# Linear attention and maxout feed-forward: keys' maximum taken off on VectorE, turned keys over two PSUM banks, order by new numbers

## The chip, the cores and the metric

One core of a Trainium2 chip. The core has TensorE (PE in the profile: matrix products and transposes; PEld is its weight load), VectorE (DVE), ScalarE (ACT), GpSimd (POOL) and SyncE (SP), which here only issues DMAs; ScalarE issues some too. The metric is the device time of one execution, in microseconds (us). The kernel before takes 657.2 us, the median of three runs (656.23 to 659.95).

## The reference

Eight batches of eight heads, 576 tokens, head size 64. Queries go through a softmax over the head's 64 columns, keys through one over the 576 tokens; then two small products per head, and a feed-forward with three gates of which the largest is kept:

```python
q_s = np.exp(q - np.max(q, axis=-1, keepdims=True))
q_s = q_s / (np.sum(q_s, axis=-1, keepdims=True) + 1e-09)
k_s = np.exp(k - np.max(k, axis=2, keepdims=True))
k_s = k_s / (np.sum(k_s, axis=2, keepdims=True) + 1e-09)
kv = np.einsum('bhsd,bhse->bhde', k_s, v)
x = np.einsum('bhsd,bhde->bhse', q_s, kv)        # 4608 tokens x 512, heads side by side
h = np.maximum(np.maximum(x @ w1, x @ w2), x @ w3)   # d_ff 768
return (h @ w_out).astype(np.float32)
```

q, k and v are float32; the four weights arrive as float64.

## The kernel before

**Stages.** Tokens are worked on in chunks of 512 columns. A product of float32 accuracy is made of three float32r products of a high and a low part (line 972: low by high, high by low, high by high). Chunks 0 to 2 run plain (`Chunk`, gates at line 973, second layer at 1012); the other six go in three duos that save products by adding blocks first (`Duo`, lines 1149 and 1260). The weights come as twelve slices of 1 MB. Each slice is turned from float64 into high and low parts by a run of steps (`Slice`): line 510 or 508, 512, 514 and 518 on VectorE (the first may go to ScalarE), 541 and 537 on ScalarE, 532 on GpSimd, 551 on VectorE or GpSimd. A gate needs its slice split and its chunk's x.

**Attention.** `Pair` is two heads of a batch, so 32 pairs. Batches 0 and 1 (eight pairs) are "turned": they run while the weights still arrive. For these, `k_turned` transposes the keys on TensorE into PSUM (L644 four blocks of 128 tokens, L650 the last 64), takes the maximum along the tokens on VectorE (L655 to L657), makes the exponentials on ScalarE with that maximum as bias (L663, L664, with the sum as a by-product), transposes them back (L671, L673), copies them out (L680), and multiplies with v (L722, ten products of 64x64). The result, scaled by one over the sum (L728, L731), is written into two diagonal blocks of a 128x128 tile `bdf` (L734). Queries are normalized in rows (L748 to L801), transposed (L830), copied out (L835), and L846 makes x for 512 columns as one 128x512 product. L854 and L856 split x into high and low parts. The other 24 pairs are "plain" (`k_plain`, `Quad`), with lines 687 to 707 and 880 to 929; they run beside the gates.

**PSUM.** Seven banks of 512 columns are handed out by the planner; the eighth, `ps`, is cut in quarters that take turns for the last 64 keys (L650), the last block of the turned-back exponentials (L673), the product with v (L722) and others.

**Order.** Every engine executes its own list of instructions in order. The lists are written by a planner (`Streams`), which runs through the steps of all parts by a cost for each step and a rank; tables of numbers at the head of the file (`LATE`, `AT`, `Q_OFF` and so on) are the ranks. Where the planner sees TensorE idle for more than 0.35 us in the first 110 us of its own clock, it writes fillers: products of 128x128 with the identity whose result nobody reads (L460), about one per 0.26 us of that gap (`fill`). The numbers of the fillers are therefore fixed when the program is written. `Q_BY_ACT` names the pairs whose query exponentials ScalarE makes row group by row group (L764, eight for a turned pair) in place of a subtraction on VectorE (L769), one exponential (L793) and a sum on VectorE (L795).

Of the kernel before, what the change touches and what calls it, by code (L numbers as in the profile page):

```python
# [48 lines left out]
SLICES_AT = -84.14
SLICE_STEP = 134.98  # L50
SLICE_HI = -258.29
SLICE_LO = 126.09
GATES_AT = -85.68
FIRST_LOADS = 'kqKkwqvqvKqkvVwvVk'
FIRST_ON_ACT = 9
LEFT_AT = -128.94
ROOMS = 2, 2, 2, 2

Q_BY_ACT = (1, 2, 6, 7, 8, 9, 10, 11, 12, 14, 17, 18, 20, 24, 25, 27, 31)

PLAIN = 3
FIRST_BANKS = 5
# [63 lines left out]
def dve_reduce(n):  # L126
    return (n + 140) / 960


def act(n):  # L130
    return n / 1200 + 0.12
# [181 lines left out]
def linear_attention_then_maxout_ffn(  # L313
# [48 lines left out]
    ps = ctx.enter_context(tc.tile_pool(name="ps", bufs=1, space=PSUM))  # L362
# [20 lines left out]
    banks = [pf.tile([P, CH], F32, name=f"bank{i}") for i in range(7)]  # L383
# [12 lines left out]
    bdf = [start.tile([P, P], F32, name=f"bdf{i}", bufs=1) for i in range(TURNED * NP)]  # L396
    qbuf = [start.tile([P, 2, 4, D], F32, name=f"q1{i}", bufs=1) for i in range(2)]

# [13 lines left out]
    for i in reversed(range(TURNED * NP)):  # L412
        nc.gpsimd.memset(bdf[i], 0.0)
    for i in range(2):
        nc.gpsimd.memset(vbuf[i][:, :, :, D:NV], 1.0)
        nc.gpsimd.memset(vbuf[i][LEFT:P, :, 4, :], 0.0)
# [15 lines left out]
    def banks_of_heads(key):  # L432
        return (4, 5, 6) if key[-1] < NP * (PLAIN + 2) else range(7)
# [4 lines left out]
    for d in range((B + 1 - PLAIN) // 2):  # L438
# [3 lines left out]
        {"pf": banks_of_gates, "pa": banks_of_heads, "ring": RING, "ws": 1, "sums": 1, "vs": 1, "halves": 2, "ps": 4, "keT": ROOM_KET, "hp": NJ, "tmp": N_TMP, "ke": 2, "qe": ROOM_QE, "qf": ROOM_QF, "qt": 2, "tb": N_TB, "qT": N_QT},  # L442
# [23 lines left out]
    class Slice:  # L466
# [35 lines left out]
        def join(self, room):  # L502
            n, low, high = self.n, self.low, self.high
            e = yield Step("AV", (1.0, 0.67), [("wst", n)], take=[(room, n)], port="V")
# [6 lines left out]
            yield Step("V", 0.67, port="V")  # L511
            nc.vector.tensor_scalar(out=x, in0=x, scalar1=HIGH_LEAST, scalar2=HIGH_MOST, op0=ALU.max, op1=ALU.min)
# [53 lines left out]
    class Pair:  # L566
# [70 lines left out]
        def k_turned(self):  # L637
# [9 lines left out]
            if n == 0:  # L647
                filler(0, 7, 1.0)
# [931 lines left out]
```

## Time and profile before

| | |
|---|---|
| median of 3 runs | 657.2 us (656.23 to 659.95) |
| profiled execution: span from first to last instruction | 653.8 us; the median of the runs is 3.4 us more |
| TensorE busy | 642.4 us (98%), 3594 matmul records |
| VectorE busy | 452.2 us (69%) |
| ScalarE busy | 289.5 us (44%) |
| GpSimd busy | 58.7 us (9%) |
| DMA | 140.64 MB, 215 GB/s in the mean |
| granted TensorE clock, mean | 0.997 |

The profile gives no time of the profiled execution other than its span, so what lies around the span is the difference to the runs: 2.4 to 6.1 us. A busy engine in the profile is one that runs an instruction; fillers count as busy. A float32 product is recorded as two matmuls, a float32r product or a transpose as one. The mean of a matmul is longer than its share of the time because matmuls overlap; the chain of waits gives each its own share.

### The profile page before, as it was taken

The numbers are of one execution on the slowest core, as the hardware profiler recorded it, in microseconds if no ns is written. First come the engines' busy times: TensorE is split into PE (matmuls) and PEld (weight loads), VectorE is DVE, ScalarE is ACT, GpSimd is POOL, SyncE is SP. The second block draws the span as 40 slices with busy tenths as digits, with TensorE's granted clock in tenths as the row PEclk, the third lists the DMA queues.
The fourth block names the chain that finished last, engine by engine and source line by source line (L and its number), as shares of the span: only waits on it lengthen the run. The fifth ranks groups of instructions, "written<-read, shape, count | busy, mean of one in ns | idle before, by whom it ended". The sixth has DMA issues, their size and how long they took to land.

```text
span 653.8 us, 9984 instructions
## 1 busy us (share of the span) xinstructions
PE 642.4 (98%) x3594; PEld 520.8 (80%) x3594; DVE 452.2 (69%) x788; ACT 289.5 (44%) x728; POOL 58.7 (9%) x72
## 2 busy tenths in 40 slices
PE   9899999999999999999999999999999999999997
PEld 9678778888777787777877787888888888888885
DVE  7899778688998898998999792253548614444521
ACT  5877584377663774664535354111113421111132
POOL 1322433201010100000000000000000000000000
PEclk9899999999999999999999999999999999999999
DMA  8999994378879997888997853466650536663012
GB/s 249 280 313 319 293 361 153 108 248 264 260 258 320 334 285 254 279 290 249 310 304 233 254 191 115 148 208 186 195 181 20 190 117 202 186 204 112 0 66 64
DMA packets 97953, 140.64 MB, mean 215 GB/s; under 512 B 28656, under 2 KB 57072, under 8 KB 96752
## 3 DMA queue, kind: packets, MB, share of 16 engines
q1 hardware_dynamic: 93008, 134.31, 65.5%
q10 hardware_dynamic: 4896, 5.70, 2.9%
q8 instruction: 28, 0.46, 0.3%
q14 instruction: 21, 0.17, 0.1%
HBM read 102.24 MB, written 37.75 MB: 214 GB/s over the span
## 4 chain that ended last, share of the span: by engine, by line
PE 79%; DMA 10%; DVE 6%; ACT 2%; issue 2%; SPq 1%; DVEq 0%; ACTq 0%
PE bank L1149 36%; PE bank L973 15%; PE bank L1260 15%; PE bank L1012 4%; DMA scratch<-bench 3%; DMA turned<-tb 2%; PE ps L880 1%; PE bank L460 1%; DMA wst<-in_moe_w_dram 1%; PE ps L722 1%; DMA kt<-in_k_dram 1%; PE bank L846 1%; DVE tb L806 1%; DMA gw<-scratch 1%; PE bank L929 1%
## 5 line engine op out<-in xcount | busy, mean ns | idle before, releaser
L1149 PE MATMUL bank<-gw 128*128 128x512 f32 x1134 | 261.3, 390 | 1.9 <-DMA gw<-scratch 1.3
L1149 PEld LDWEIGHTS bank<-gw 128*128 128x128 f32 x1134 | 212.1, 188 | 51.2 <-DMA gw<-scratch 2.1
L973 PE MATMUL bank<-gw 128*128 128x512 f32 x432 | 103.3, 395 | 0.0
L973 PEld LDWEIGHTS bank<-gw 128*128 128x128 f32 x432 | 80.2, 188 | 20.0 <-issue 3.6
L1260 PE MATMUL bank<-oh,halves 128*128 128x512 f32 x288 | 88.7, 389 | 0.0
L1260 PEld LDWEIGHTS bank<-oh,halves 128*128 128x128 f32 x288 | 54.1, 188 | 11.2
L1260 PE MATMUL bank<-ol,halves 128*128 128x512 f32 x144 | 56.3, 391 | 0.0
L973 PE MATMUL bank<-x,gw 128*128 128x512 f32 x216 | 50.1, 390 | 0.0
L973 PEld LDWEIGHTS bank<-x,gw 128*128 128x128 f32 x216 | 40.4, 188 | 9.2 <-issue 0.8
L1238 DVE TENSOR_TENSOR halves<-hf,halves 128x768 fp32r<-128x768 f32 (+2 forms) x30 | 23.7, 794 | 34.2 <-ACT halves L1236 34.2
L1012 PE MATMUL bank<-oh,h 128*128 128x512 f32 x144 | 44.4, 389 | 0.0
L782 ACT ACTIVATE qt<-qt,qm 128x64 f32<-128x64 f32 x117 | 39.2, 337 | 3.0 <-DVE qm L777 2.7
L1211 ACT COPY m<-bank 128x512 f32<-128x512 f32 x18 | 10.6, 588 | 61.7 <-PE bank L1149 59.2
L694 POOL PARTITION_ALL_REDUCE kma<-kh x24 | 18.9, 789 | 204.7 <-DVE ke L700 102.1
L1279 ACT COPY m<-bank 128x512 f32<-128x512 f32 x23 | 13.5, 589 | 52.4 <-PE bank L1260 52.4
L1260 PEld LDWEIGHTS bank<-ol,halves 128*128 128x128 f32 x144 | 27.0, 188 | 7.2 <-issue 0.8
L1206 ACT COPY m<-bank 128x512 f32<-128x512 f32 x18 | 10.6, 588 | 48.7 <-PE bank L1149 48.7
L985 DVE TENSOR_TENSOR m<-bank,m 128x512 f32<-128x512 f32 x36 | 24.7, 685 | 10.7 <-PE bank L973 7.9
L1012 PEld LDWEIGHTS bank<-oh,h 128*128 128x128 f32 x144 | 27.0, 188 | 5.6
L806 DVE STREAM_TRANSPOSE tb<-qt 128x576 f32<-128x576 f32 x24 | 30.4, 1273 | 0.1
L1213 DVE TENSOR_TENSOR m<-bank,m 128x512 f32<-128x512 f32 x18 | 12.4, 690 | 25.9 <-PE bank L1149 25.4
L1012 PE MATMUL bank<-ol,h 128*128 128x512 f32 x72 | 28.3, 393 | 0.0
(164 smaller groups left out, 883.4 us busy)
## 6 DMA issues: line engine op xcount, KB each, us to landing
gw<-scratch SPq DMA_DIRECT2D x75, 512.0 KB, 3.9
gw<-scratch SPq DMA_DIRECT2D x39, 256.0 KB, 3.7
wst<-in_moe_w_dram SPq DMA_DIRECT2D x9, 1024.0 KB, 7.1
scratch<-bench SPq DMA_DIRECT2D x9, 1024.0 KB, 5.3
out_dram<-m SPq DMA_DIRECT2D x32, 256.0 KB, 2.3
scratch<-gw SPq DMA_DIRECT2D x27, 256.0 KB, 3.4
qt<-in_q_dram SPq DMA_DIRECT2D x24, 288.0 KB, 4.3
kt<-in_k_dram SPq DMA_DIRECT2D x24, 256.0 KB, 4.8
```

What stands on the lines that cost most here:

```text
L694: nc.gpsimd.partition_all_reduce(kma, kmv.rearrange("p h d -> p (h d)"), P, bass_isa.ReduceOp.max)
L782: nc.scalar.activation(out=rows3[:, i, :], in_=rows3[:, i, :], func=AF.Exp, bias=qm[:, i : i + 1], accum_out=sums[:, i, 0:1],)
L806: nc.vector.transpose(out=tb.rearrange("p e (c s) -> p s e c", s=QS), in_=self.qt.rearrange("p s (c e) -> p s e c", e=2))
L973: nc.tensor.matmul(out=ps, lhsT=l[:, cc], rhs=r, start=(cc == 0 and t == 0), stop=(cc == NC - 1 and t == 2))
L985: nc.vector.tensor_max(out=m, in0=self.m.pop((j, i)), in1=m)
L1012: nc.tensor.matmul(out=po, lhsT=l, rhs=r[:, j, :], start=(j == 0 and i == 0), stop=(j == NJ - 1 and i == 2))
L1149: nc.tensor.matmul(out=po, lhsT=w[:, a, cc], rhs=x[:, b, cc], start=(first and cc == 0 and t == 0), stop=(cc == 1 and t == 2), skip_group_ ...
L1206: nc.scalar.copy(out=mb, in_=po("v"))
L1213: nc.vector.tensor_sub(out=ma, in0=po("w"), in1=ma)
L1238: nc.vector.tensor_sub(out=hl, in0=src, in1=hh.bitcast(F32))
L1260: nc.tensor.matmul(out=po, lhsT=l, rhs=r[:, j, :], start=(j == 0 and i == 0), stop=(end and i == 2))
L1279: nc.scalar.copy(out=o, in_=po)
```

## The change

- **Keys of a turned pair.** `KEYS_LESS` names the seven of eight pairs for which the maximum no longer becomes the bias of exponentials in the turned layout. After the turn and the maximum (one reduction over 576 columns), TensorE spreads the maximum over all partitions (L669: the maximum as a broadcast weight times the identity), VectorE subtracts it from the keys in token rows (L673, 128x640, in1 from PSUM), and ScalarE makes one exponential of 640 columns (L678). The transposes back and the copies out are gone for these. The sums come from five products with a column of ones (L739).
- **PSUM.** The eight banks are one tile, `psum`. The turned keys lie in one stretch of 576 columns, all of bank 6 and 64 columns of bank 7, always there; the product with v and the sums take banks 4 or 5. Filler, `ps` quarters and the rest are as before.
- **x.** `bdf` is 128x64, both heads' blocks below each other, written by one ScalarE instruction (L757). x is made by two products of 64x512 (L877). For three pairs (`X_LESS`) the low part of x is made on TensorE by subtracting the high part (L888) and a ScalarE copy, in place of VectorE's subtraction.
- **Slices.** The step at line 523 (512 before) may go to GpSimd.
- **Order.** All tables of ranks, `Q_BY_ACT` (turned pairs 0, 2 to 7 in place of 1, 2, 6, 7; fifteen plain pairs in place of thirteen), the order of the first loads, the banks and several costs of the planner are new. 57 fillers are written in place of 92.

```diff
-FIRST_LOADS = 'kqKkwqvqvKqkvVwvVk'
+FIRST_LOADS = "KqqkwKVkvvqvkVvqwk"
-FIRST_BANKS = 5
+FIRST_BANKS = 4
+HEADS_ON = 4, 5
+KEYS_LESS = (1, 1, 1, 1, 1, 1, 1, 0)
+X_LESS = (0, 1, 0, 1, 1, 0, 0, 0)
 def act(n):
-    return n / 1200 + 0.12
+    return n / 1200 + 0.07
...
+    turning = psum[:, 6 * CH : 6 * CH + S]
+    quarters = psum[:, 7 * CH :].rearrange("p (a b) -> p a b", a=4)
...
-            yield Step("V", 0.67, port="V")
-            nc.vector.tensor_scalar(out=x, in0=x, scalar1=HIGH_LEAST, scalar2=HIGH_MOST, op0=ALU.max, op1=ALU.min)
+            e = yield Step("VG", (0.61, 1.1), port="VG")
+            unit[e].tensor_scalar(out=x, in0=x, scalar1=HIGH_LEAST, scalar2=HIGH_MOST, op0=ALU.max, op1=ALU.min)
...
+            less = KEYS_LESS[n]
+            room = [("pa", ("kT", n)), ("last", ("kT", n))]
+            yield Step("T", 0.74, [("k", n)], take=room + ([] if less else [("keT", n)]), gives=None if less else ("ksub", n))
...
+            yield Step("V", dve_reduce(S), free=room[1:] if less else ())
+            km = att.tile([P, 1], F32, name="km2", bufs=4)
+            nc.vector.tensor_reduce(out=km, in_=turning, op=ALU.max, axis=AX.X, negate=not less)
+            if less:
+                yield Step("T", 0.25)
+                kb = turning[:, :P]
+                nc.tensor.matmul(out=kb, lhsT=km.broadcast_to([P, P]), rhs=ident, start=True, stop=True)
+                yield Step("V", dve(640), take=[("ke", n)], free=room[:1], gives=("ksub", n))
...
+                    op=ALU.subtract,
+                )
+                yield Step("A", act(640))
+                nc.scalar.activation(out=ke, in_=ke, func=AF.Exp)
+                return
...
+            if less:
+                yield Step("T", 0.35, [self.ago("xmm", 0)], take=last, gives=("sum", n))
+                kv = banks[st.bank(*last[0])]
+                for s in range(5):
+                    rows = slice(0, LEFT if s == 4 else P)
+                    nc.tensor.matmul(
+                        out=kv[:, D:NV], lhsT=ke[rows, s].rearrange("p h d -> p (h d)"), rhs=ones[rows],
+                        start=(s == 0), stop=(s == 4),
+                    )
...
-            nc.tensor.matmul(out=xT, lhsT=self.terms[0], rhs=self.terms[1], start=True, stop=True)
-            yield from x_words(b, self.g, xT, room)
+            less = bool(X_LESS[n])
+            for r in heads:
+                nc.tensor.matmul(
+                    out=xT[r], lhsT=self.terms[0][r], rhs=self.terms[1][r], start=True, stop=not less,
+                    skip_group_check=less,
+                )
...
+            yield Step("T", f32r(CH))
+            nc.tensor.matmul(out=xT, lhsT=minus, rhs=h, start=False, stop=True, skip_group_check=True)
```

How the lists read now, at three places. TensorE before, from behind the first turned query to the first x (`ps` takes the last keys and the product with v):

```order
L460 MATMUL bank_81<-ident 128x128 x13
L644 MATMUL bank_85<-ident,k_99 128x128 x4
L650 MATMUL ps<-ident,k_99 128x64
L460 MATMUL bank_81<-ident 128x128 x8
L722 MATMUL ps<-v_101,ke 64x64 x10
L671 MATMUL bank_86<-ident,keT 128x128 x4
L673 MATMUL ps<-ident,keT 64x128
L644 MATMUL bank_87<-ident,k_99 128x128 x4
L650 MATMUL ps<-ident,k_99 128x64
L460 MATMUL bank_81<-ident 128x128 x5
L846 MATMUL bank_85<-qf,bdf_102 128x512
```

and the same stretch of the change (`km` is the maximum, `zero` and `ident` with L471 the fillers):

```order
L859 MATMUL psum<-ident,qe 128x128 x4
L471 MATMUL psum<-ident 128x128
L657 MATMUL psum<-ident,k_90 128x128 x4
L657 MATMUL psum<-ident,k_90 128x64
L471 MATMUL psum<-ident 128x128 x3
L739 MATMUL psum<-ones,ke 128x1 x5
L752 MATMUL psum<-v_92,ke 64x64 x10
L471 MATMUL psum<-ident 128x128 x7
L669 MATMUL psum<-ident,km_329 128x128
L471 MATMUL psum<-ident 128x128
L877 MATMUL psum<-qf,bdf_93 64x512 x2
```

The transposes back (L671, L673) are gone, the spread of the next pair's maximum and the five sums are there, and the fillers between the first turned query and the first x fell from 26 to 12. Before that query stand 27 fillers before and 28 now.

VectorE before, from the first maximum of the keys on (`left<-wst` is the first weight slice):

```order
L655 TENSOR_REDUCE km_247<-bank_85 128x1
L656 TENSOR_REDUCE km_247<-ps 128x1
L657 TENSOR_SCALAR km_247<-km_247 128x1
L795 TENSOR_REDUCE qs<-qe 128x8
L797 TENSOR_REDUCE qr_145<-qs 128x8
L798 RECIPROCAL qr_145<-qr_145 128x8
L801 TENSOR_TENSOR qe<-qe,qr_145 128x512
L510 TENSOR_SCALAR left<-wst 128x1024
```

and of the change:

```order
L665 TENSOR_REDUCE km_241<-psum 128x1
L826 TENSOR_REDUCE qr_130<-qs 128x8
L827 RECIPROCAL qr_130<-qr_130 128x8
L824 TENSOR_REDUCE qs<-qe 128x8
L521 TENSOR_SCALAR left<-wst 128x1024
L830 TENSOR_TENSOR qe<-qe,qr_130 128x512
L523 TENSOR_SCALAR left<-left 128x1024
L673 TENSOR_TENSOR ke<-k_90,psum 128x640
```

The first step of the slice (L521) now stands ahead of the first pair's query scaling (L830) and of its key subtraction (L673); before, the query scaling (L801) stood ahead of the slice.

TensorE before, around the fourth x and the first keys of batch 1 (`kt`):

```order
L644 MATMUL bank_86<-ident,kt_92 128x128 x4
L650 MATMUL ps<-ident,kt_92 128x64
L846 MATMUL bank_85<-qf,bdf_105 128x512
L460 MATMUL bank_83<-ident 128x128 x8
L973 MATMUL bank_83<-gw 128x512 x3
L973 MATMUL bank_81<-gw 128x512 x3
L973 MATMUL bank_82<-gw 128x512 x3
L973 MATMUL bank_83<-gw 128x512 x9
L973 MATMUL bank_84<-gw 128x512 x12
```

and of the change:

```order
L877 MATMUL psum<-qf,bdf_96 64x512 x2
L657 MATMUL psum<-ident,kt_82 128x128 x4
L657 MATMUL psum<-ident,kt_82 128x64
L1016 MATMUL psum<-gw 128x512 x6
L888 MATMUL psum<-gw,minus 128x512
L471 MATMUL psum<-ident 128x128 x2
L669 MATMUL psum<-ident,km_590 128x128
L471 MATMUL psum<-ident 128x128
L739 MATMUL psum<-ones,ke 128x1 x5
L752 MATMUL psum<-vt_85,ke 64x64 x10
L1016 MATMUL psum<-gw 128x512 x6
```

Before, a run of 66 gate products follows here and batch 1's keys come later; now batch 1's pairs go on at once, with gates between them in sixes. When the last turned x is issued, 180 gate products lie behind it before and 96 now.

## Rows read from the trace of the kernel before

**Rows 1.** Stages: length; PE, PEld, DVE, ACT, POOL busy (instructions); clock; DMA; GB/s.

```profile
0.00:10.00 10.00, 8.93 (x58) 8.74 (x59) 7.07 (x23) 3.19 (x7) 2.02 (x17) 1.00 0.77 233
10.00:20.00 10.00, 7.44 (x70) 7.01 (x70) 8.63 (x17) 8.80 (x38) 2.54 (x2) 0.96 1.00 306
20.00:42.00 22.00, 21.93 (x176) 16.52 (x174) 19.54 (x42) 17.36 (x41) 6.96 (x6) 0.94 0.95 266
42.00:60.00 18.00, 18.00 (x93) 15.09 (x93) 16.77 (x27) 10.87 (x17) 4.44 (x4) 1.00 1.06 373
60.00:101.00 41.00, 39.65 (x268) 31.82 (x268) 33.27 (x65) 30.48 (x80) 15.13 (x12) 1.00 0.94 310
101.00:130.00 29.00, 29.00 (x140) 24.27 (x139) 21.98 (x32) 10.10 (x14) 9.49 (x10) 1.00 0.32 108
130.00:270.00 140.00, 140.00 (x917) 111.41 (x916) 122.90 (x246) 88.12 (x277) 11.79 (x14) 1.00 0.87 278
270.00:380.00 110.00, 108.07 (x648) 84.86 (x648) 100.08 (x178) 54.94 (x152) 6.35 (x9) 1.00 0.90 270
```

**Rows 2.** Groups on TensorE, 0 to 101 us: busy, mean ns, idle before.

```profile
L973 PE MATMUL bank<-gw 128*128 128x512 f32 x181 | 44.7, 400 | 0.0
L460 PE MATMUL bank<-ident 128*128 128x128 f32 x168 | 22.1, 280 | 0.0
...
L460 PE MATMUL bank<-bdf 128*128 128x128 f32 x16 | 3.8, 431 | 1.1 <-POOL bdf L413 1.1
```

**Rows 3.** Waits of TensorE, 0 to 101 us: total, times, longest.

```profile
PE ps L722 <- ACT keT L664: 2.6, 1, 2.6
PE ps L722 <- DVE km L656: 1.2, 3, 0.5
PE bank L460 <- POOL bdf L413: 1.1, 1, 1.1
```

**Rows 4.** Chain of waits: start us, us, what (x: records).

```profile
37.43 2.74 PE bank L973 x12
...
58.66 0.44 PE bank L671 x4
59.10 0.11 PE ps L673
...
60.95 0.95 PE ps L722 x20
...
69.19 1.53 PE bank L460 x12
...
86.60 0.86 PE bank L846 x2
```

**Rows 5.** TensorE in order of time: first key turn; a plain pair's x.

```profile
4.64 1.06 PE L644 MATMUL bank<-ident,k 128*128 128x128 f32 x4
...
208.19 1.09 PE L929 MATMUL bank<-qT,bd 64*64 64x64 f32 x10
```

**Rows 6.** VectorE in order of time: the first slice step.

```profile
11.20 0.69 DVE L510 TENSOR_SCALAR left<-wst 128x1024 uint32<-128x1024 uint32 x1 [1.42 <-DMA wst<-in_moe_w_dram]
```

**Rows 7.** Groups on VectorE by form (L700 over the whole span).

```profile
L518 DVE SCALAR_TENSOR_TENSOR left<-wst,left 128x1024 uint32<-128x1024 uint32 x6 | 7.6, 1273 | 0.0
L801 DVE TENSOR_TENSOR qe<-qe,qr 128x512 f32<-128x512 f32 x8 | 6.3, 791 | 0.0
...
L655 DVE TENSOR_REDUCE km<-bank 128x1 f32<-128x512 f32 x8 | 5.4, 670 | 0.1
L512 DVE TENSOR_SCALAR left<-left 128x1024 f32<-128x1024 f32 x7 | 4.8, 685 | 0.0
...
L700 DVE TENSOR_TENSOR ke<-kt,kma 128x640 f32<-128x640 f32 x24 | 19.4, 809 | 0.0
```

**Rows 8.** Groups on ScalarE and GpSimd by form, 0 to 101 us.

```profile
L764 ACT ACTIVATE qe<-q,qm 128x64 f32<-128x64 f32 x32 | 10.7, 338 | 0.0
...
L532 POOL TENSOR_TENSOR m<-left,wst 128x512 int32<-128x512 int32 x12 | 15.7, 1326 | 36.2 <-DVE left L518 13.2 <-ACT bdf L734 10.9 <-DMA kt<-in_k_dram 5.8
```

More of the change, by code (lines that the diff above doesn't have):

```diff
@@ L382, in linear_attention_then_maxout_ffn @@
     wholes = dram.tile([NG // 2, P, 2, CH], F32, name="wholes")
-    banks = [pf.tile([P, CH], F32, name=f"bank{i}") for i in range(7)]
+    psum = pf.tile([P, 8 * CH], F32, name="psum")
+    banks = [psum[:, i * CH : (i + 1) * CH] for i in range(7)]
     ident = const.tile([P, P], F32, name="ident")
@@ L395, in linear_attention_then_maxout_ffn, with flat_keys @@
     v0 = early.tile([P, H, 5, D], F32, name="v0")
-    bdf = [start.tile([P, P], F32, name=f"bdf{i}", bufs=1) for i in range(TURNED * NP)]
+    bdf = [start.tile([P, D], F32, name=f"bdf{i}", bufs=1) for i in range(TURNED * NP)]
+    zero = start.tile([P, P], F32, name="zero", bufs=1)
     qbuf = [start.tile([P, 2, 4, D], F32, name=f"q1{i}", bufs=1) for i in range(2)]
+    def flat_keys(t):
+        return t.rearrange("p h s d -> p (h s d)").rearrange("p (s h d) -> p s h d", s=5, h=2)
     nc.vector.memset(ones, 1.0)
@@ L411, in linear_attention_then_maxout_ffn @@
         )
-    for i in reversed(range(TURNED * NP)):
-        nc.gpsimd.memset(bdf[i], 0.0)
+    minus = start.tile([P, P], F32R, name="minus", bufs=1)
+    nc.vector.tensor_scalar(out=minus, in0=ident, scalar1=-1.0, scalar2=None, op0=ALU.mult)
+    nc.gpsimd.memset(zero, 0.0)
+    nc.gpsimd.memset(k0[LEFT:P, 4], 0.0)
     for i in range(2):
-        nc.gpsimd.memset(vbuf[i][:, :, :, D:NV], 1.0)
-        nc.gpsimd.memset(vbuf[i][LEFT:P, :, 4, :], 0.0)
+        nc.gpsimd.memset(flat_keys(kbuf[i])[LEFT:P, 4], 0.0)
     def main_rows(src, b, hs):
@@ L516, in join @@
             )
[L517 removed]
+            yield Step("V", 1.15, gives=("or", n), port="V")
             nc.vector.scalar_tensor_tensor(
@@ L639, in k_turned @@
             n, kt = self.n, self.kt
-            rooms = [("pa", ("kT", n)), ("ps", ("kTl", n))]
-            yield Step("T", 0.74, [("k", n)], take=rooms + [("keT", n)], gives=("ksub", n))
-            kT = banks[st.bank("pa", ("kT", n))]
-            for s in range(4):
+            less = KEYS_LESS[n]
[3 more added lines that the diff above has]
+                rows = slice(0, LEFT if s == 4 else P)
@@ L668, in k_turned @@
+            yield Step("A", act(S) + 0.2, free=room, gives=("sum", n))
+            keT = start.tile([P, S], F32, name="keT", bufs=ROOM_KET)
+            self.sums = start.tile([P, 1], F32, name=f"ks{n}", bufs=1)
+            nc.scalar.activation(out=keT, in_=turning, func=AF.Exp, bias=km, accum_out=self.sums)
+            rooms = [("pa", ("ke", n)), ("last", ("kel", n))]
             yield Step("T", 0.56, take=rooms + [("ke", n)], free=[("keT", n)])
@@ L714, in k_steps @@
                 return
-            ke = self.ke
-            last = [("ps", ("kv", n))]
-            yield Step("T", 0.9, [("v", n), self.ago("xmm", 0)], take=last, free=[("ke", n)], gives=("kv", n))
-            kv = next(small)
+            ke, less = self.ke, KEYS_LESS[n]
+            last = [("pa", ("kv", n))]
+            if less:
+                yield Step("T", 0.35, [self.ago("xmm", 0)], take=last, gives=("sum", n))
+                kv = banks[st.bank(*last[0])]
+                for s in range(5):
+                    rows = slice(0, LEFT if s == 4 else P)
+                    nc.tensor.matmul(
+                        out=kv[:, D:NV], lhsT=ke[rows, s].rearrange("p h d -> p (h d)"), rhs=ones[rows],
+                        start=(s == 0), stop=(s == 4),
+                    )
+                self.sums = kv[:, D:NV]
+            yield Step(
+                "T", 0.9, [("v", n), self.ago("xmm", 0)], take=[] if less else last, free=[("ke", n)], gives=("kv", n)
+            )
+            if not less:
+                kv = banks[st.bank(*last[0])]
             for s in range(5):
```

128 lines of the change are left out of this document (65 added, 63 removed).

## The prediction

> **What bounds the kernel now.** I read the stages first. From 101 to 270 us TensorE is busy without a gap, and from 270 to 380 it lacks 1.9 us [rows 1]; there the time is the number of products, and the change neither adds nor removes a gate product or a plain pair. Idle TensorE stands at the start: of the first 101 us it is busy 95.95, so 5.05 us are lost. The waits name them [rows 3]: 1.1 us for the first tile, 2.6 us at the first product of keys with v, put down to ScalarE's exponentials of the *next* pair (L664), and 1.2 us in three waits of the same product for VectorE's maximum of the last 64 keys (L656). These exponentials and maxima read other quarters of the PSUM bank that the product writes; the product does not need their data.
>
> But busy isn't useful. The groups of the first 101 us [rows 2] hold 25.9 us of fillers (22.1 and 3.8), which only stand where the planner saw a gap. So some 31 us of the first 101 are waiting of one kind or the other. Gates have 181 records; at 2.74/12 = 0.228 us of the chain each [rows 4] that is 41.3 us, and 101 - 41.3 - 25.9 - 5.05 = 28.7 us are left for the eight turned pairs. All the change can save lies in the 31 us of waiting and these 28.7 us. After 101 us it can only disturb.
>
> **The change part by part.** Each term goes against the profiled execution (span 653.8 us; the runs' median of 657.2 us is 3.4 more, which I keep).
>
> *Fillers.* 57 in place of 92, counted in the two lists. Six take 1.53 us in the chain [rows 4], 0.255 each: 35 x 0.255 = -8.9 us. This is only a gain where the wait behind them is gone too; real waits are a term of their own below.
>
> *Turned keys.* Seven pairs lose four transposes back (0.44) and the last block (0.11) [rows 4]: -3.9 us. They gain one product that spreads the maximum (128 columns, float32, as a filler: 0.255): +1.8. They gain five sums of one column. No row has such a shape. Its bounds are a 64x64 product, 0.95/10 = 0.095 us, and a filler with the same 128x128 weight, 0.255 [rows 4]; I take the transposes' 0.11, the nearest with a full weight: 35 x 0.11 = +3.9 (3.3 to 8.9).
>
> *x.* Three subtractions by product: 3 x 0.228 = +0.7. The two 64x512 halves in place of one 128x512 product use different quarters of the array. For a plain pair four such 64x512 products and one small one end within 1.09 us [rows 5], against 0.86 for one full float32 product [rows 4], so halves do run beside each other: 0. The bound is 0.86 more per pair.
>
> Work on TensorE together: -3.9 + 1.8 + 3.9 + 0.7 = +2.5 us.
>
> *Other engines.* VectorE is busy 78.2 of the 91 us from 10 to 101, ScalarE 67.5 [rows 1], so their sums matter. VectorE per turned pair: the maximum in one instruction saves two small ones, about 0.3, and the subtraction of 640 adds 0.81 [rows 7]: +0.5 x 7. Less: three low parts of x (0.7 each), three more queries by ScalarE (two operations of 0.7), three slice steps to GpSimd (0.685 each [rows 7]): -8.4. Sum about -5 us. ScalarE gains three queries at 8 x 0.338 = 2.7 [rows 8] less 0.6, and loses exponentials, copies back and one of two scalings in seven or eight pairs: about -2 us. Both get a little lighter: 0, hidden under TensorE. The three GpSimd steps are bounded by VectorE's 0.685 and twice GpSimd's 512-column addition, 2.65 us [rows 8]; the next step of that slice waits for it, but not the gates, of which only 96 are asked for by the last turned x, against 180 before. I cost it at 0; without that cover it is up to 3 x 2 = 6 us.
>
> *ScalarE's queue at the start.* It now issues five loads; two wait for an earlier load to land, and the first eight query exponentials stand behind them. The result is wanted only behind the first slice step on VectorE, which starts at 11.20 [rows 6]. Hidden: 0, at worst about 1.
>
> *Waits that go.* The product with v has a bank of its own: the 2.6 and the 1.2 us [rows 3] lose their cause. What is late next is worked out along the lists:
> - First turned query. VectorE's list has the slice step (11.20 to 11.89 [rows 6]) ahead of the query scaling (0.79 [rows 7]): ready at 12.7. TensorE turns the first keys at 4.64 [rows 5], 1.3 us with the last block, then comes 20 fillers and the spread later, 21 x 0.255 = 5.4: at about 11.3. Wait 1.4.
> - Second keys' turn. It overwrites the bank from which VectorE subtracts the first maximum, after a slice step: 12.7 + 0.69 + 0.81 = 14.2 [rows 7]. TensorE is there at 12.7 + 0.44 + 0.26 = 13.4. Wait 0.8.
> - Third. Between the two subtractions VectorE has one slice step of 0.69, one of 1.27, a query scaling 0.79, two reductions 1.4 [rows 7], small ones 0.7, two splits of 0.8 and the subtraction: 7.3 us, to 21.5. TensorE has from 14.2 on 14 fillers (3.6), turn, sums, product with v, spread, x and query, 0.65 + 0.55 + 0.95 + 0.255 + 0.86 + 0.44: 21.5 less what waits in between. Wait 0.7 with the spread's own.
> - Later turns in the same way: of the five left I take 3.3 us together, the largest at batch 1's first pair, whose turn stands straight behind the fourth x.
>
> With 1.1 at the start: 7.3 us, against 5.05: +2.2. First x should be out at about 20 us.
>
> *Steady part.* The first plain product stands behind 381 gate products in both lists. VectorE is busy 123 of 140 us there [rows 1], and two more of 24 plain queries go to ScalarE. The new order could remove the 1.9 us or double it: 0, bounds -2 and +4.
>
> Sum: -8.9 + 2.5 + 2.2 = -4.2 us. 657.2 - 4.2 = **653.0 us**. Ends, each alone: sums at the filler's price +5, halves one after another +6.9, GpSimd +6, steady part -2 to +4, waits at zero after the start -6.2.
>
> **The rivals.**
>
> *The wait stays, only the fillers go.* The 35 fillers stood for gaps the planner saw; its new costs may simply see shorter ones. For it: the 2.6 us wait of before was not planned, and VectorE at 86% leaves it little to catch up with. Against: the transposes back and their copies, two steps of the chain of each pair, are really gone. Half of the 8.9 us coming back as idle gives 657.4.
>
> *More overlap than I count.* If the turns find VectorE ahead, the waits shrink to the 1.1 and 1.4, 2.5 in place of 7.3 (-4.8), and the steady part gives its 1.9: 653.0 - 6.7 = 646.3. For it: VectorE gets 5 us lighter. Against: subtraction and maximum of a pair are now two stops in its list where there was one.
>
> *One bank for all turned keys (slower).* Before, L644 took one of several banks (87 and 86 in the lists above); now each turn waits until VectorE has subtracted for the pair before, behind whatever slice work is listed ahead. If each of seven waits holds a slice run of 0.685 + 0.685 + 1.27 = 2.64 us [rows 7], that is 18.5 in place of my 4.8: 666.7. It decides from 1.8 us a turn (4.8 + 7.5 over seven), where the sum passes 660.5. For it: the last of the lists has a turn straight behind x. Against: VectorE's list puts the subtraction near the front each time.
>
> *The halves of x take turns (slower).* Both halves now write one bank, on different partitions; in the plain pairs' rows each row half has a bank of its own, so those rows don't show this case. 8 x 0.86 = +6.9, and about 1.7 for the last 64 queries: 661.6. The Trainium skill (TensorEngine Tiling (Array Packing), Gotcha 1: PSUM Pressure) says that different row tiles cannot access one PSUM bank at the same time. By that rule this rival holds, and the sum would be that 661.6; no row of before shows it, since there the row tiles write to different banks.
>
> **How the numbers follow.** A run can be told from no change beyond about 0.5%: below 653.9 is faster, above 660.5 slower. My forecast 0.46 (own range 649.5 to 656, 0.29 of it faster, 0.17 same); waits stay 0.18 (same); more overlap 0.22 (faster); one bank 0.08 and halves 0.06 (slower). Faster 0.51, same 0.35, slower 0.14. The range of 8 in 10 is 645.5 to 660.5: it takes in the two cases beside the forecast and leaves out the slower ones and a little below.
>
> **What would show it.** Fillers near 14.5 us in the groups. The first x near 20 us. No wait of the product with v for another pair's maximum or exponentials; in their place waits of the key turn (L657) for L673 of the pair before, under 2 us each. The last turned x near 80 us, with 96 gate records ahead of it. The five sums at 0.55 us a pair in the chain, the x halves at 0.86. After that no idle TensorE beyond 2 us up to 380. It would be wrong if TensorE's idle in the turned stage passes 14 us, if the halves take 1.7 us, or if a gate waits for a slice whose step went to GpSimd.

## The result: 1.1% slower, outside the forecast

The changed kernel takes 664.9 us (median of four runs, 663.5 to 666.0) against 657.1 (656.2 to 660.0), a ratio of 1.011 [1.008, 1.013]. The forecast was 653.0 us, range 645.5 to 660.5. The profiled span is 664.1 us, 653.8 before; the median lies 0.8 us above the span here and 3.3 us before, so 2.5 us of the 10.3 us in the spans are not in the medians. Wherever the runs list both, an execution takes 1.7 to 1.9 us more than its own span (2.9 once), so the distance is not the 2.4 to 6.1 us assumed earlier: the profiled execution was a fast one before (about 655.6 us) and a slow one now (665.9). Two of the ten executions of e4 and one of the ten of e10 were more than 1.5% slower than the fastest of their kernel and are left out of the medians below.

The stages, as in [rows 1] (length; PE, PEld, DVE, ACT, POOL busy with instructions; clock; DMA share; GB/s):

```profile
0.00:10.00 10.00, 3.79 (x16) 3.49 (x16) 5.39 (x18) 1.49 (x2) 1.32 (x9) 1.00 0.81 236
10.00:20.00 10.00, 8.91 (x56) 8.40 (x57) 4.48 (x9) 4.82 (x20) 0.00 (x0) 1.00 0.89 259
20.00:42.00 22.00, 22.00 (x211) 17.98 (x211) 19.15 (x37) 17.79 (x64) 7.59 (x6) 1.00 0.64 188
42.00:60.00 18.00, 17.25 (x132) 12.89 (x127) 13.86 (x27) 13.78 (x32) 12.40 (x7) 1.00 0.89 280
60.00:101.00 41.00, 38.04 (x205) 26.69 (x203) 30.28 (x51) 28.52 (x68) 17.38 (x10) 0.96 0.86 284
```

Against [rows 1] two things stand out. In the first 10 us TensorE is busy 3.79 us, not 8.93. From 20 to 42 us the DMA engines move 188 GB/s, not 266, although VectorE and ScalarE are as busy as before. The waits of TensorE over the whole span (total, times, longest), which answer to [rows 3]:

```profile
PE psum L657 <- DMA k<-in_k_dram: 6.2, 1, 6.2
PE psum L877 <- ACT qf L864: 2.8, 1, 2.8
PE psum L1192 <- DVE m L1260: 2.1, 1, 2.1
PE psum L1192 <- DVE gw L1123: 1.1, 1, 1.1
PE psum L471 <- POOL zero L421: 1.1, 1, 1.1
PE psum L657 <- DVE ke L673: 0.3, 1, 0.3
PE psum L859 <- DVE qe L830: 0.3, 1, 0.3
```

The waits of the product with v are gone, as forecast. In their place TensorE waits 6.2 us for the first keys, which the forecast took as landed at 4.6 us [rows 5], and 2.8 us at the seventh x. TensorE in order of time (idle before in brackets):

```profile
11.08 1.09 PE L657 MATMUL psum<-ident,k 128*128 128x128 f32 x4 [6.23 <-DMA k<-in_k_dram]
11.96 3.19 PE L471 MATMUL psum<-ident 128*128 128x128 f32 x14
...
25.53 1.08 PE L877 MATMUL psum<-qf,bdf 64*64 64x512 f32 x4
...
84.58 1.97 PE L877 MATMUL psum<-qf,bdf 64*64 64x512 f32 x4 [2.84 <-ACT qf L864]
...
120.55 0.39 PE L1055 MATMUL psum<-ol,h 128*128 128x512 f32 x1
```

The first x is out at 25.5 us (forecast 20). The last row is the first product of the second layer. In both kernels it stands behind the same 216 gate products and all turned pairs, so the start can be compared there. (The prediction's 381, up to the first plain pair, are 309 gate products and 72 of the second layer in both.) Before:

```profile
111.32 0.39 PE L1012 MATMUL bank<-ol,h 128*128 128x512 f32 x1
```

The loss is thus 9.2 us at this point, and 1.1 us of the remaining 542 to 544 us. The table splits the 9.2. Each instruction counts from its start to the next start, less the idle in brackets; the columns are sums of such rows.

| up to the second layer, us | before | changed | difference | forecast |
|---|---|---|---|---|
| fillers | 24.05 | 17.92 | -6.1 | -8.9 |
| transposes back (one pair left) | 4.82 | 0.64 | -4.2 | -3.9 |
| spreads of the maximum | 0 | 1.73 | +1.7 | +1.8 |
| sums of one column | 0 | 8.62 | +8.6 | +3.9 |
| x | 6.38 | 8.98 | +2.6 | 0 |
| low part of x on TensorE | 0 | 0.78 | +0.8 | +0.7 |
| product with v | 7.59 | 6.84 | -0.8 | 0 |
| gates | 51.28 | 52.46 | +1.2 | 0 |
| left queries' x | 1.70 | 1.07 | -0.6 | 0 |
| turning keys and queries | 10.67 | 10.77 | +0.1 | 0 |
| idle | 4.83 | 10.74 | +5.9 | +2.2 |
| sum | 111.32 | 120.55 | +9.2 | -4.2 |

The groups of TensorE up to 101 us (busy, mean ns, idle before), which answer to [rows 2]:

```profile
L1016 PE MATMUL psum<-gw 128*128 128x512 f32 x135 | 36.2, 409 | 0.0
L471 PE MATMUL psum<-ident 128*128 128x128 f32 x98 | 15.9, 305 | 0.0
L877 PE MATMUL psum<-qf,bdf 64*64 64x512 f32 x32 | 9.6, 672 | 2.8 <-ACT qf L864 2.8
L739 PE MATMUL psum<-ones,ke 128*128 128x1 f32 (+1 forms) x70 | 9.1, 248 | 0.1
```

A filler is longer on average (305 ns, 280 before), in part since seven of them run slowly after the long first wait: the 14 records at 11.96 took 3.19 us, where 14 took 1.73 at 17.30. The chain of waits prices the sums (start, us, what):

```profile
57.08 1.10 PE psum L739 x10
58.17 0.88 PE psum L752 x20
...
69.80 7.89 DMA scratch<-gw
77.71 4.31 DMA m<-in_q_dram
...
90.47 1.01 PE psum L877 x4
```

Five sums are 1.10 us here and 1.23 on average (8.62/7): 0.246 each, what a filler costs (1.73/7). An undisturbed x is 1.01 us. The two DMA pieces lead to the wait at 84.58: the load of the left queries was issued behind writes of split weights. The x behind that wait took 1.97 us, at the lower granted clock:

```profile
84.20:87.60 3.40, 3.02 (x7) 1.21 (x8) 3.40 (x6) 2.04 (x4) 0.00 (x0) 0.50 0.89 283
```

Why the weights come late from 20 to 42 us is seen on SyncE, which issues most loads. Its wait for one line up to 101 us, and its issues around it:

```profile
SPq L633 <- DMA vt<-in_v_dram: 19.3, 4, 7.5
```

```profile
33.85 0.59 SPq L631 DMA_DIRECT2D vt<-in_v_dram  x1
39.50 0.62 SPq L633 DMA_DIRECT2D vt<-in_v_dram  x1
40.22 0.54 SPq L570 DMA_DIRECT2D wholes<-m  x1
40.94 0.37 SPq L503 DMA_DIRECT2D wst<-in_moe_w_dram  x1
```

L631 loads the first 512 tokens of v for two heads, L633 the last 64. L633 stands until L631 has landed, and every issue behind it with it, among them the fourth weight slice (40.94; 33.30 before). No such wait exists before. The change rewrote this load (one DMA for two heads into a new layout of the tile), and the forecast had no term for it.

### The profile page after: what moved, and what is told of

Same layout as the page of the kernel before. It is cut to its first block, busy times and chain, and to the rows that moved or that the text cites. A ratio compares the mean times of both kernels' runs of the same rounds, so it can differ in the third digit from the quotient of the medians.

```text
span 664.1 us, 10046 instructions
## 1 busy us (share of the span) xinstructions
PE 645.3 (97%) x3608; PEld 518.6 (78%) x3608; DVE 443.7 (67%) x759; ACT 293.7 (44%) x770; POOL 74.3 (11%) x71
## 4 chain that ended last, share of the span: by engine, by line
PE 75%; DMA 8%; DVE 6%; ACT 1%; issue 1%; ACTq 0%; SPq 0%; DVEq 0%
PE psum L1192 37%; PE psum L1016 16%; PE psum L1303 15%; DMA scratch<-bench 4%; PE psum L1055 2%; PE psum L923 2%; PE psum L972 1%; DMA qt<-in_q_dram 1%; DMA scratch<-gw 1%; DMA m<-in_v_dram 1%; DVE tb L835 1%; DMA m<-in_q_dram 1%; PE psum L877 1%; DVE gw L1123 1%; DVE raw L1119 1%
## 5 line engine op out<-in xcount | busy, mean ns | idle before, releaser
L1192 PE MATMUL psum<-gw 128*128 128x512 f32 x1134 | 260.8, 390 | 3.2 <-DVE m L1260 2.1
L1192 PEld LDWEIGHTS psum<-gw 128*128 128x128 f32 x1134 | 212.2, 188 | 51.8 <-issue 3.2
L1016 PE MATMUL psum<-gw 128*128 128x512 f32 x432 | 105.2, 397 | 0.1
L1016 PEld LDWEIGHTS psum<-gw 128*128 128x128 f32 x432 | 79.7, 189 | 22.6 <-issue 3.2
L1303 PE MATMUL psum<-oh,halves 128*128 128x512 f32 x288 | 88.7, 389 | 0.0
L1303 PEld LDWEIGHTS psum<-oh,halves 128*128 128x128 f32 x288 | 54.1, 188 | 11.2
L1303 PE MATMUL psum<-ol,halves 128*128 128x512 f32 x144 | 56.2, 391 | 0.0
L1016 PE MATMUL psum<-x,gw 128*128 128x512 f32 x216 | 49.7, 390 | 0.0
L1016 PEld LDWEIGHTS psum<-x,gw 128*128 128x128 f32 x216 | 40.4, 188 | 9.2 <-DVE tb L835 0.8
L1055 PE MATMUL psum<-oh,h 128*128 128x512 f32 x144 | 44.4, 389 | 0.0
L1254 ACT COPY m<-psum 128x512 f32<-128x512 f32 x18 | 10.5, 585 | 56.0 <-PE psum L1192 51.1
L1322 ACT COPY m<-psum 128x512 f32<-128x512 f32 x23 | 13.5, 588 | 48.0 <-PE psum L1303 48.0
L1249 ACT COPY m<-psum 128x512 f32<-128x512 f32 x18 | 10.6, 587 | 47.7 <-PE psum L1192 46.1
L1028 DVE TENSOR_TENSOR m<-psum,m 128x512 f32<-128x512 f32 x36 | 24.6, 684 | 10.4 <-PE psum L1016 9.4
L1256 DVE TENSOR_TENSOR m<-psum,m 128x512 f32<-128x512 f32 x18 | 12.4, 691 | 27.5 <-PE psum L1192 27.3
```

Of the source, the lines that this page charges most:

```text
L1016: nc.tensor.matmul(out=ps, lhsT=l[:, cc], rhs=r, start=(cc == 0 and t == 0), stop=(cc == NC - 1 and t == 2))
L1028: nc.vector.tensor_max(out=m, in0=self.m.pop((j, i)), in1=m)
L1055: nc.tensor.matmul(out=po, lhsT=l, rhs=r[:, j, :], start=(j == 0 and i == 0), stop=(j == NJ - 1 and i == 2))
L1192: nc.tensor.matmul(out=po, lhsT=w[:, a, cc], rhs=x[:, b, cc], start=(first and cc == 0 and t == 0), stop=(cc == 1 and t == 2), skip_group_ ...
L1256: nc.vector.tensor_sub(out=ma, in0=po("w"), in1=ma)
L1303: nc.tensor.matmul(out=po, lhsT=l, rhs=r[:, j, :], start=(j == 0 and i == 0), stop=(end and i == 2))
```

## Experiments

Two theories stood against each other. **Loads:** data arrive late because of how loads are issued (first keys, then everything behind the loads of v). **VectorE's list:** the steps on VectorE, or the one bank for the turned keys, set the pace, and earlier data only wait elsewhere. "Mark" is the start of the second layer, "idle" TensorE's idle up to it; the ratio is to executions of the kernel before taken beside each run.

| run | us | ratio to before [95%] | span | mark | idle |
|---|---|---|---|---|---|
| changed kernel | 664.9 | 1.011 [1.008, 1.013] | 664.1 | 120.55 | 10.74 |
| e1 keys first | 665.7 | 1.012 [1.009, 1.015] | 663.6 | 123.56 | 10.38 |
| e2 slice later | 658.4 | 1.001 [0.999, 1.004] | 658.7 | 117.54 | 6.72 |
| e3 before, late keys | 662.1 | 1.007 [1.004, 1.009] | 658.8 | 116.81 | 10.19 |
| e4 keys first, one sum | 660.4 | 1.003 [1.000, 1.006] | 660.6 | 117.54 | 11.29 |
| e5 v apart | 657.6 | 1.001 [0.999, 1.002] | 656.0 | 115.02 | 7.28 |
| e6 slice later, v apart | 653.9 | 0.994 [0.992, 0.996] | 650.7 | 110.27 | 4.63 |
| e7 and keys first | 657.6 | 1.000 [0.997, 1.002] | 652.6 | 110.56 | 4.04 |
| e8 and two sums | 655.5 | 0.998 [0.996, 0.999] | 656.0 | 112.83 | 6.59 |
| e9 is e6 again | 654.1 | 0.995 [0.992, 0.997] | 650.5 | 110.82 | 3.83 |
| e10 and half the fillers | 656.1 | 0.997 [0.994, 0.999] | 654.7 | 110.40 | 5.53 |
| e11 and sums of half width | 651.3 | 0.990 [0.986, 0.993] | 649.1 | 108.09 | 4.23 |
| e12 both halves | 651.8 | 0.991 [0.987, 0.995] | 651.9 | 110.13 | 6.59 |

Span, mark and idle are of one execution each. Those of e2, e8 and e12 were slow ones of their kernel (2.1, 2.4 and 3.0 us above the median), that of e7 a fast one (3.2 us below), so differences of marks of up to 3 us say little by themselves.

**e1: the first keys issued first.** In the changed kernel the loads at the start go out as left keys of two heads (0), two queries (1, 2), first keys of two heads (3, 4), weight slice (5), and so on, by turns on SyncE and ScalarE. The edit permutes them (slot i, on its own queue, issues load `order[i]`) and leaves all compute lists as they are:

```diff
+        order = (3, 4, 0, 1, 2, 5)
...
```

> The changed kernel with the first six loads in another sequence (first pair's keys on both queues at once, then last keys, queries, weight slice); the lists of all compute engines are unchanged. Theory A: the changed kernel loses most of its time because TensorE waits 6.2 us for the first keys (they land at 11.1 in place of 4.6), and runs its next products slowly for some 2 us. Then the first key turn begins before 6.5 us and the time falls by 6 to 8.5 us, to 656.5 to 659. Rival B: the opening is hidden, because VectorE, ScalarE and the weight slices set the pace of the first 100 us; the wait then turns up again further on and the time stays at 663 to 665.

The keys were there in time, and the time did not fall. VectorE of this run:

```profile
10.60 0.69 DVE L777 TENSOR_REDUCE qm<-q 128x8 f32<-128x512 f32 x1 [5.17 <-DMA q<-in_q_dram]
11.32 0.69 DVE L798 TENSOR_TENSOR qe<-q,qm 128x512 f32<-128x512 f32 x1
11.93 0.75 DVE L665 TENSOR_REDUCE km<-psum 128x1 f32<-128x576 f32 x1
```

Now the queries land late (10.6), and in VectorE's list the keys' maximum (L665) stands behind them. TensorE waits 3.6 us at L669 in place of 6.2 us at L657, and 1.4 us more at the first query. That is not all: behind these waits most of the stretch up to 29.8 us ran at the lower granted clock:

```profile
12.80:16.10 3.30, 3.30 (x15) 3.30 (x16) 0.71 (x3) 3.30 (x18) 0.00 (x0) 0.50 1.00 265
19.60:29.80 10.20, 10.20 (x58) 9.17 (x59) 5.71 (x13) 4.27 (x19) 2.75 (x2) 0.50 0.59 165
```

The same part of TensorE's list, from the fillers behind the second keys' turn to the second turned query, took 10.5 us here (from 19.92) and 6.1 in the changed kernel (from 20.49), without a wait in either. The mean granted clock was 0.984 to 0.993 in all six executions, against 0.990 to 0.997. So e1 does not show that late keys are free: with the queries late in their place, a wait and a lower clock took the gain back.

**e2: the slice issued five loads later,** keys and queries as in the changed kernel. The slice thereby also moves from ScalarE's queue to SyncE's, behind the keys (4.26 us).

```diff
+        order = (0, 1, 2, 3, 4, 6, 7, 8, 9, 10, 5)
...
```

> The changed kernel with its first weight slice issued five loads later; queries still go ahead of the first keys. Of the first keys' lateness: if the 1 MB slice beside them holds them up (A1), the first key turn begins by 6 to 7.5 us; if the queries ahead of them do (A2), it still begins at 9.5 to 11. The time itself tells little, since the slice comes 4 to 6 us later and VectorE's list has its first step ahead of the first subtraction: 658 to 668 either way.

```profile
6.71 1.09 PE L657 MATMUL psum<-ident,k 128*128 128x128 f32 x4 [1.86 <-DMA k<-in_k_dram]
...
20.48 1.08 PE L877 MATMUL psum<-qf,bdf 64*64 64x512 f32 x4
...
47.46 0.79 PE L888 MATMUL psum<-gw,minus 128*128 128x512 f32 x1 [3.52 <-ACT gw L886]
```

The key loads are issued at the same times (1.22 us on ScalarE, 2.15 on SyncE); the first lands 0.6 us earlier, the second 4.4. So it is the 1 MB slice, issued on ScalarE's queue at 1.95, that held the second up. Before, the slice stood behind the keys in SyncE's queue. The keys come in packets of 256 bytes, the slice in packets of 2 KB. From 6.0 to 7.5 us of the changed kernel 205 packets of the first kind ran on SyncE's queue beside 225 of the second on ScalarE's, nearly one for one; in e2, ahead of the slice, SyncE's queue ran 1,276 of 256 bytes from 5.0 to 6.5 us. The Trainium skill (DMA: Bandwidth & Descriptors, Queues, rings and completion order) says that each DMA engine takes turns between the queues a whole packet at a time. These counts agree, though in e3 below the keys got fewer turns than that (64 beside 191 from 5.5 to 7.0 us). Whether a slice issued as late on ScalarE's queue would have done as well was not tried. The time falls by 6.5 us, and the first x is at 20.5. A new wait of 3.5 us is left at 47.5: ScalarE's list waits for a slice that went out at 38.68, behind L633.

**e3: the kernel before with the changed sequence of first loads** (numbered as in the kernel before).

```diff
+        order = (3, 2, 7, 0, 1, 6, 4, 5)
...
```

> The kernel before with its first loads issued in the changed kernel's sequence (last keys, two queries, first keys, slice); its compute lists are unchanged. Theory A: TensorE's first key turn moves from 4.6 to about 11 us and the time rises by 5 to 8 us, to 662 to 665. Rival B: it stays within 2 us of 657.

```profile
10.45 1.08 PE L644 MATMUL bank<-ident,k 128*128 128x128 f32 x4 [5.96 <-DMA k<-in_k_dram]
```

The first key turn moves from 4.64 [rows 5] to 10.45, and the old kernel loses 5.0 us. That is the price of the sequence alone, in that kernel.

**e4: as e1, with four of the five sum products left out.** It leaves out part of the keys' sums.

```diff
-                for s in range(5):
...
+                nc.tensor.matmul(
+                    out=kv[:, D:NV], lhsT=ke[:, 0].rearrange("p h d -> p (h d)"), rhs=ones, start=True, stop=True
+                )
```

> As the keys-first kernel, and of the five products with the column of ones only the first is issued for each of the seven pairs, so the key sums are left out in four parts of five. If a one-column product costs what a filler costs (0.25 us, theory A), 28 of them are 7 us and the time is 6 to 8 us below the keys-first kernel; if it costs a transpose's 0.11 us (the prediction's value), 2.5 to 3.5 us below; if the stage is set by VectorE and ScalarE (rival B), within 1 us of it.

The mark comes 6.0 us earlier than in e1, the medians differ by 5.3 us with a wide spread of runs (655 to 664). 28 products at 0.246 would be 6.9, at the transposes' 0.11 3.1. The result lies between the two expectations, nearer to the first, so most of their price seems real, even where other waits stand.

**e5: v in two blocks,** on the changed kernel alone: the first 512 tokens of both heads, then the last 64.

```diff
-                    self.vt = flat[:, : 2 * 5 * D].rearrange("p (h s d) -> p h s d", h=2, s=5)
+                    self.vm = flat[:, : 2 * 4 * D].rearrange("p (h s d) -> p h s d", h=2, s=4)
+                    self.vl = flat[:, 2 * 4 * D : 2 * 5 * D].rearrange("p (h d) -> p h d", h=2)
...
```

> Edit, on the changed kernel alone: for the four turned pairs of batch 1 v lies as one block of the first 512 tokens of both heads and one block of the last 64, in place of five row groups per head. In the changed kernel the second load of v (L633) stands on SyncE until the first (L631) has landed, 19.3 us in four waits up to 101 us, and the weight slices queued behind it go out at 30.5 and 40.9 us (22.9 and 33.3 before). Theory A (late data: first keys, then slices held up on SyncE's queue): these four waits go to nearly 0, the third and fourth slice go out 4 to 7 us earlier, the moved bytes from 20 to 42 us rise from 188 to over 240 GB/s; but TensorE still waits 6.2 us for the first keys. TensorE's wait of 2.8 us at the sixth x may go: 664.9 - 2 to 5 = 660 to 663. Theory B (VectorE's list and the one bank for the turned keys set the pace, the queue is hidden): the SyncE waits go and the time stays at 664 to 666.

SyncE's issues:

```profile
30.14 0.59 SPq L632 DMA_DIRECT2D vt<-in_v_dram  x1
30.78 0.70 SPq L634 DMA_DIRECT2D vt<-in_v_dram  x1
35.14 0.34 SPq L570 DMA_DIRECT2D wholes<-m  x1
36.38 0.37 SPq L503 DMA_DIRECT2D wst<-in_moe_w_dram  x1
```

L634 (L633) follows at once, and of the four waits 0.3 us is left; the fourth slice is issued at 36.38. From 20 to 42 us the DMA engines move 232 GB/s in place of 188, a little less than expected. The time falls by 7.3 us, more than the 2 to 5 expected, although TensorE still waits 5.6 us for the first keys. At the mark 5.5 us are won, 3.5 of them idle (the 2.8 at the seventh x among them, the "sixth" of the expectation), the rest mostly x and gates, which had run slowly after that wait; beyond it another 2.6, of which 2.0 are waits at the later products (3.2, now 1.2). The list theory (664 to 666) falls.

**e6 and e9: both edits.**

> Edit: the first weight slice issued five loads later (as in the experiment that took 658.4), and v of batch 1 in two blocks. There one large wait was left, 3.5 us at 47.5 us for ScalarE's high part of a gate input (L886), which stood behind a slice issued at 38.7 us, behind two SyncE waits of v's second load (5.4 and 5 us). Theory A: this wait goes, and with it the lower granted clock of 42 to 60 us (0.72): 658.4 - 3.5 - 1 to 2 = 653 to 655. Theory B (VectorE's list): the wait moves to another instruction of the same stretch and the time stays at 657 to 659.

> The kernel with the first weight slice five loads later and v of batch 1 in two blocks once more, beside the kernel before and the three below, for a narrower interval. Theory A (both loads were the cause of the loss): 653.9 again, ratio to the kernel before 0.993 to 0.996. Theory B (the first reading was a lucky draw of four runs): above 0.998.

TensorE's waits in e9:

```profile
PE psum L658 <- DMA k<-in_k_dram: 1.9, 1, 1.9
PE psum L471 <- POOL zero L421: 1.1, 1, 1.1
PE psum L658 <- DVE ke L674: 0.6, 2, 0.3
PE psum L1194 <- ACT m L1218: 0.3, 1, 0.3
PE psum L861 <- DVE qe L832: 0.3, 1, 0.3
```

Both readings agree: 654, which is 0.5% below the kernel before and 10.9 us below the changed one. The edits alone win 6.5 and 7.3; they don't add up (10.9, not 13.8), perhaps since each also lets part of the other's delay be caught up, which no run shows. Of VectorE's list 0.9 us of waiting is left (2.0 in e6's profile), and 0.6 of it is the bank for the turned keys.

**e7: also the keys first.**

> As the run before it, with the two key loads also issued first of all, ahead of the left keys and the two queries. Theory A: first key turn at 4.7 us in place of 6.7, so the 1.9 us wait goes; but the queries come later by about one load each (0.6 to 1.2 us), and in the run with keys first alone VectorE's list (query reductions ahead of the maximum) gave the gain back. So 0 to -2 us against the run before: 652 to 655. Theory B: the opening is set by VectorE's list, whose first entries are the queries; keys first makes them late: +1 to +3 us against the run before.

The 1.9 us at the keys went, and TensorE waits 1.9 us longer for the first query in their place (L861 for L832: 2.2, against 0.3 in e9). The mark of the profiled execution, the fastest of ten, is the same within 0.3 us. The median is 3.7 us above e6's, and the two intervals don't overlap, so keys first are a loss here, a little more than the second theory's +1 to +3. The four executions with a mean granted clock of 0.991 or less took 656.8 to 661.6 us, the other six 654.4 to 658.1; e6's four had 0.997 to 1.000. So part of the loss goes with the clock; none of these longer executions was profiled.

**e8: GpSimd adds four blocks of exponentials, TensorE sums two in place of five,** behind the product with v.

```diff
+                nc.gpsimd.tensor_add(out=half, in0=ke[:, 0:2], in1=ke[:, 2:4])
+                nc.gpsimd.tensor_add(out=half[:, 0], in0=half[:, 0], in1=half[:, 1])
...
```

> As the slice-later, v-apart run, with the sums of seven pairs made otherwise: GpSimd adds the four full blocks of the exponentials to one (two additions of 256 and 128 columns), and TensorE sums two blocks in place of five, behind the product with v. 21 one-column products fewer. Theory A (each takes 0.25 us of the chain, as a full weight does, not the 0.11 of the forecast): 21 x 0.25 = -5.2 us, less what TensorE waits for GpSimd (0 to 2 us in all): 648 to 651 if the run before takes 654. Theory B (TensorE's time at the start only fills the gaps that VectorE leaves, so cheaper sums become idle): less than 1.5 us, and TensorE's idle up to 101 us rises by 3 us or more.

The sums fall from 8.63 to 4.77 us up to the mark, but TensorE waits for the additions, and the mark comes 2.6 us later:

```profile
PE psum L755 <- POOL half L682: 3.2, 3, 2.1
```

The first theory had 0 to 2 us for this wait, and so expected a gain; the median is 1.5 us above e6's. The idle grew by 2.0 us, not by the second theory's 3. Beside the wait, the granted clock was 0.81 from 42 to 60 us (1.00 in e6), and the profiled execution was the slowest of ten.

**e10: every burst of n identity fillers cut to (n+1)/2.**

```diff
-        for _ in range(n):
+        for _ in range((n + 1) // 2 if t else n):
...
```

> The kernel of the run above with every burst of n identity fillers cut to (n+1)/2: 49 become 30, 19 x 0.23 us = 4.3 us of fillers fewer. Theory A (as the forecast took it: a filler is time of TensorE, and its removal is a gain where the loads are in time): -2 to -4 us, idle of TensorE up to the second layer grows by less than 2 us from 4.6. Theory B (the fillers stand where VectorE's list makes TensorE wait anyway): idle grows by about 4 us, to 8 to 9 us, the time stays within 1 us, or gets longer by 1 to 2 us where the granted clock falls.

Fillers fall from 17.07 (e9) to 13.63 us up to the mark. Half of that comes back as idle (3.83 to 5.53) and some in slower instructions: the granted clock is 0.95 from 10 to 20 us and 0.92 from 20 to 42, 1.00 in e9. The mark is 0.4 us earlier, and later waits (1.9 and 1.4 us for VectorE) take more than that back. The median is 2 us above e9's, so cutting fillers did not pay here.

**e11: each sum as two products of 64 columns of weights; e12: with e10.**

```diff
+                    for hh, r in enumerate(heads):
+                        nc.tensor.matmul(
+                            out=kv[r, D:NV], lhsT=ke[rows, s, hh, :], rhs=ones[rows], start=(s == 0), stop=(s == 4)
+                        )
...
```

> The kernel of the first run of this call with each of the five one-column sums (128 columns of weights) made as two products with 64 columns of weights, one per head. Theory A (a one-column product costs what its weights cost: 0.246 us with 128 columns, and 0.088 as the 64x64 products with v do, 0.88 for ten): 1.23 us a pair becomes 0.88, 7 x 0.35 = -2.4 us of TensorE's time, and 1 to 2.4 us of the whole. Theory B (a fixed price of each product, whatever its weights): ten in place of five double it, +8.6 us of TensorE's time, +4 to +8 us.

> The two edits above together. Theory A: -3 to -6 us against the first run of this call: 648 to 651. Theory B: what is saved becomes waiting for VectorE: 653 to 655.

Ten such products take 0.77 us of the chain where five of full width took 1.23:

```profile
49.93 0.77 PE psum L741 x20
50.70 0.88 PE psum L753 x20
```

7 x 0.46 = 3.2 us is the difference of the sums up to the mark too (8.63 to 5.40), and the time falls by 2.7 to 651.3: the best of all runs, 1.0% below the kernel before. A fixed price for each product would have doubled the 1.23. In the trace the matmul records of the full-width sums start 0.112 us apart; those of the halves start in pairs, the two heads 7 ns apart, with a pair every 0.058 us. So the two heads run side by side, and a record with half the columns of weights takes half the time. Half the fillers on top win nothing.

## Why the forecast was wrong

- **The step that failed: the first loads.** "ScalarE's queue at the start ... Hidden: 0, at worst about 1", with the first key turn taken over from before at 4.64 us. The new sequence puts a 1 MB slice beside the keys, on the other queue; the turn comes at 11.08. e2 (issue times of the keys unchanged, turn at 6.71, 6.5 us won) and e3 (the old kernel loses 5.0 us) show it.
- **A step that was not there: the load of v.** The list of what the change moves had no line for v's new layout and its single DMA. Four waits of SyncE, 19.3 us, delay the slices and the left queries; e5 gives 7.3 us back. The forecast priced a queue at the start only, and ScalarE's alone.
- **Sums mis-sized.** +3.9 by the transposes' 0.11 became +8.6; the upper bound, 0.255 a product (+8.9), was right. A transpose is one matmul record, a float32 sum is two (x10 for five), 0.112 us apart: the forecast took the price of one record for two. Of the two nearest rows the filler, with the same weights and also two records, was the better guide.
- **Fillers.** -8.9 became -6.1, for the number was right and each filler longer (0.31 us, 0.26 before). As the rival "the wait stays" supposed, e10 shows half of the time of the fillers cut returning as idle.
- **x.** 0 became +2.6: 0.2 us a pair (1.01 against 0.80) and 0.9 from the one at 84.58, at the lower clock.
- **VectorE's waits were over-forecast:** 6.2 us expected at turns and queries, 0.6 measured, and 0.9 where the loads are mended. So "one bank for all turned keys" is refuted although it named nearly the measured time (666.7): its key turns wait 0.3 us in all for L673.
- **"The halves of x take turns" is refuted.** One after another they would be 1.72 us; they take 1.01 in the chain, in one bank, and their records start 7 ns apart (25.532 and 25.539 us at the first x). The rule of the Trainium skill (TensorEngine Tiling (Array Packing), Gotcha 1: PSUM Pressure), that row tiles cannot access one bank at the same time, does not hold for these two halves, which write different partitions of the bank.
- **Right:** the transposes back, the spreads, the low part of x, the waits of the product with v, 35 fillers fewer. With both loads mended the kernel runs at 654, near the forecast of 653.0, but that is luck in part: its sums cost 4.7 us more than forecast and its waits less.
- **Two signs for later stages failed:** the last turned x came at 90.4 us (forecast near 80), and TensorE lacked 3.3 us from 130 to 380 us (at most 2).

## What to carry to other kernels

When an edit touches loads, write down for each load what stands beside it on the other queue and what stands behind it on its own; a wait on an issuing engine delays data that look unrelated and shows first as fewer GB/s in a stage where TensorE is fully busy. A point that all versions reach after the same work (here the second layer) splits a loss into idle and price per group at once. Small products are priced from a row with the same weights and the same number of matmul records for a product.

## What the hardware showed unexpectedly

A load in packets of 256 bytes, issued at 2.15 us, landed 4.4 us later because of a 1 MB load in packets of 2 KB that ran beside it on the other queue. And the clock: after the idle of 3.5 us at 47 us in e2 the granted clock is 0.50 (the lower of its two levels, 1.2 GHz) from 47.4 to 56 us, with TensorE busy nearly throughout; these are its stages from 44 us on:

```profile
44.00:47.40 3.40, 0.00 (x0) 0.00 (x0) 0.29 (x1) 1.59 (x3) 0.38 (x1) 0.93 1.13 349
47.40:52.00 4.60, 4.54 (x21) 4.42 (x23) 2.89 (x7) 4.38 (x13) 3.30 (x1) 0.50 1.03 354
52.00:56.00 4.00, 4.00 (x26) 3.16 (x27) 2.50 (x5) 2.01 (x4) 3.03 (x3) 0.50 0.79 284
```

So that wait cost more than its 3.5 us: five sums took 2.01 us there, 1.10 to 1.23 elsewhere. After the 6.2 us wait at the start of the changed kernel the rows grant 1.00, and yet the first seven fillers ran at about half speed. In e5 the same seven, after a wait of 5.6 us, took the same 3.19 us from 11.35 on, and there the row shows the lower level:

```profile
11.35:14.50 3.15, 3.15 (x16) 2.92 (x15) 0.00 (x0) 3.01 (x17) 0.00 (x0) 0.50 0.97 248
```

e3 is alike (3.10 us at 0.50, after 6.0 us). The first clock record in the changed kernel's trace is a rise to 1.00 at 15.95 us, so its 1.00 ahead of that stands for no record. Most likely, then, the lower clock slowed these fillers too.
